# The softmax's division in a fused attention and two-MoE kernel: GpSimd's scaling of the exponentials against factors spread by TensorE

## The chip, the cores and the metric

The kernel runs on one core of a Trainium2 chip. The metric is device time in microseconds (us) of one execution, median of three runs. The engines are named as in the profile: PE is TensorE (PEld its weight loads), DVE is VectorE, ACT is ScalarE, POOL is GpSimd, SP is SyncE, which starts the DMAs.

## The reference

Three stages follow one another, all in float32. Attention runs over 2 batches x 12 heads x 448 positions x 64 columns with a causal mask; its output, 896 tokens of 768 columns, goes through two expert layers.

```python
scores = where(causal, q @ k.T / 8, -1e9)
attn = exp(scores - max(scores))
attn = attn / (sum(attn) + 1e-9)
x = (attn @ v), heads side by side            # 896 x 768
h = x @ w_in                                  # 768 -> 2048
x = (P(h) / (Q(h) + 1e-6)) @ w_out            # P cubic, Q quadratic; 2048 -> 768
out = (sigmoid(x @ w_gate) * (x @ w_val)) @ w_out2   # 768 -> 1536 -> 768
```

## The kernel before, in words

Attention works on 12 pairs of heads (2 batches x 6, `pairs`). A pair has 448 queries in four blocks of 112 (`NQ`), a block t against the t + 1 blocks of keys that the mask leaves; the blocks go in three groups, (0, 1), (2,) and (3,). For each block and each head j of the pair:

- `scores` (line 574): PE multiplies queries and keys into a PSUM tile s, both heads in different rows of the array.
- `maximum` (line 582): DVE adds the mask, scales, writes the tile e to SBUF and its extreme to sc.
- `exponentials` (line 596): ACT takes e to its exponential in place and the sums of the rows to `sum`.
- `inverses` (lines 602, 603): DVE adds 1e-9 to the sums of one group and takes the reciprocal, three times a pair.
- `normalised` (line 607): POOL multiplies e by its row's inverse sum, eight times a pair.
- `turn` (line 618): PE transposes e, block by block, into a PSUM tile p that shares its two buffers with s.
- `copied` (lines 626, 628): p goes to SBUF as pt, block 2 by ACT and the others by DVE.
- `values` (line 636): PE multiplies v and pt into x, 128 rows (two heads of 64 columns) x 448 queries, two PSUM buffers.
- `result_hi` (line 649) and `result_lo` (line 652): ACT rounds x to its high part xh, DVE subtracts, x - xh, to the low part xl. Every product of the expert layers is three products of high and low parts, for accuracy.

The first expert layer's products (`up`, lines 260 to 262, tile h; `out1_tile`, lines 319 to 321, tile o) begin as soon as a pair's xh and xl are there, and fill PE between the steps of attention. So do the portions of weights (`weight`: ACT lines 165 and 169, DVE line 172, POOL lines 180 and 184). What follows h is `rational` (lines 275 to 293, ACT, DVE, POOL).

The order on each engine is written out by a planner: every step is a job with an engine, a cost, the jobs it needs and a rank. `in_turn` walks through the jobs in a modelled time and lets each engine take the job of the lowest rank among those that are ready; the instructions are emitted in that order and each engine runs them in it. The tables R (ranks), C (added costs) and H (hand-over times) are numbers written into the kernel; expert products have rank 1000, so that they come where attention leaves PE free. From `late` on (all attention jobs done) the attention's memory is used for weights.

```python
job(("norm", n, t, j), "POOL", NORM[t] + C["norm"], [("inv", n, k)], rank + R["norm"], normalised, n, t, j)
deps = [("copy", n, t) for t in range(kt, NQ)] + [("x", n, kt - 1) if kt else ("lo", n - 2)]
job(("hi", n), "ACT", 0.42, [("x", n, NQ - 1)], rank + R["hi"], result_hi, n)
job(("lo", n), "DVE", 0.53, [("hi", n)], rank + R["lo"], result_lo, n)
```

Of the kernel before, what the change touches and what calls it, by code (L numbers as in the profile page):

```python
# [8 lines left out]
F32 = mybir.dt.float32  # L9
# [3 lines left out]
ALU = mybir.AluOpType  # L13
PSUM = bass.MemoryType.PSUM
# [57 lines left out]
def tile_causal_attention__moe_rational__moe_glu(  # L72
# [13 lines left out]
    nc = tc.nc  # L86


    B, NP, P, _, S = qk.shape
    CP, NQ, _, D = v.shape[2:]  # L90
# [29 lines left out]
    for i in range(N_WARM):  # L120
        nc.tensor.matmul(warm[:, : 2 * P], ones[:, :P], ones, start=True, stop=True)

    ident = const.tile([P, P], F32, name="ident")
# [4 lines left out]
        out=mask[:, S - CP :],  # L128
# [20 lines left out]
    xh = xpool.tile([P, KC, NT], F32R, name="xh")  # L149
    xl = xpool.tile([P, KC, NT], F32R, name="xl")  # L150
# [157 lines left out]
    def out1_tile(c, b, e):  # L308
# [37 lines left out]
        "p6": ("s2", "t2", "B", True),  # L346
        "p7": ("s3", "t3", "C", True),
        "p5": ("s1", "t1", "D", True),
        "p2": ("a12", "b21", "A", False),
        "p4": ("a22", "t4", "C", False),  # L350
        "p3": ("s4", "b22", "D", False),
# [110 lines left out]
    def combine(u, what):  # L462
# [11 lines left out]
        elif what == "u3":  # L474
            nc.vector.tensor_tensor(y, x, ps["C"], op=ALU.add)
        elif what == "c22":
# [3 lines left out]
        elif what == "c21":  # L480
            nc.vector.tensor_tensor(ps["C"], x, ps["C"], op=ALU.add)
        elif what == "pr1":
            nc.vector.tensor_tensor(z, z, ps["C"], op=ALU.mult)
        elif what == "c12":
# [45 lines left out]
    att = ExitStack()  # L530
    nat = att.enter_context(tc.tile_pool(name="nat", bufs=3))
    xn_p = att.enter_context(tc.tile_pool(name="xn", bufs=1))
# [1 line left out]
    pp = att.enter_context(tc.tile_pool(name="pp", bufs=2))  # L534
    st = att.enter_context(tc.tile_pool(name="st", bufs=3))
    ps_s = att.enter_context(tc.tile_pool(name="ps_s", bufs=2, space=PSUM))
    ps_x = att.enter_context(tc.tile_pool(name="ps_x", bufs=2, space=PSUM))

    pairs = [(b, hp) for b in range(B) for hp in range(NP)]
    T = {}  # L540

    GROUPS = [(0, 1), (2,), (3,)]
# [54 lines left out]
            e, e, AF.Exp, bias=d["sc"][:, t, j : j + 1], scale=-1.0, accum_out=d["sum"][:, t, j : j + 1]  # L597
        )

    def inverses(n, k):  # L600
        rs = T[n]["sum"][:, GROUPS[k][0] : GROUPS[k][-1] + 1]
        nc.vector.tensor_scalar_add(rs, rs, 1e-9)
        nc.vector.reciprocal(rs, rs)  # L603

    def normalised(n, t, j):
        e = T[n]["e", t, j]
        nc.gpsimd.tensor_scalar(e, e, T[n]["sum"][:, t, j : j + 1], 1.0, op0=ALU.mult, op1=ALU.mult)  # L607

    def turn(n, k):
        d = T[n]  # L610
# [9 lines left out]
    def copied(n, k, t):  # L620
# [6 lines left out]
        else:  # L627
            nc.vector.tensor_copy(dst, src)  # L628

    def values(n, kt):  # L630

        d = T[n]
        if kt == 0:
            d["x"] = ps_x.tile([P, 512], F32, tag="x", name=f"x_{n}")[:, :S]
        for j in range(2):
            nc.tensor.matmul(  # L636
                d["x"][j * D : (j + 1) * D, kt * CP :],
                d["v"][:, kt, j],
                d["pt"][:, j, kt * (PK + 1) : kt * PK + NQ].rearrange("p k c -> p (k c)"),
                start=(kt == 0),  # L640
                stop=(kt == NQ - 1),
            )

    def x_part(n):
        b, hp = pairs[n]
        return slice(None), hp, slice(b * S, (b + 1) * S)

    def result_hi(n):
        nc.scalar.copy(xh[x_part(n)], T[n]["x"])

    def result_lo(n):
        nc.vector.tensor_tensor(xl[x_part(n)], T[n]["x"], xh[x_part(n)], op=ALU.subtract)  # L652


    J = {}
# [1 line left out]
    def job(key, engine, cost, deps, rank, emit, *args):  # L657
        mode = MODES.get(key[0], "full") if engine == "PE" else None
        J[key] = Job(engine, cost, deps, rank, lambda: emit(*args), mode)
# [4 lines left out]
    def freed_by(ring, back=2):  # L664
        k = len(freed[ring]) - back
        return freed[ring][k] if k >= 0 else []
# [1 line left out]

    NG = len(GROUPS)
    LA = 2  # L670
    R = dict(s=-28.0, turn=-8.0, x=31.0, w=-6.0, max=-13.0, copy=-9.0, inv=-12.5, lo=20.0, norm=-12.0, hi=2.5, exp=8.25, e=2.0, p1=0.0, ts=0.0, th=0.0, tl=2.0, wh=-3.0, w2=-2.0, sum=-0.5)
    C = dict(w_at=14.0, w_step=6.0, s=0.05, p=-0.08, x=-0.03, max=0.05, exp=0.07, switch=0.19, stay=0, norm=0.0, copy=0.12, wa=-0.02)
    H = dict(PE=0.19, DVE=0.13, ACT=0.14, POOL=0.15, SP=0.15)
    MODES = {"s": "rows", "x": "columns"}
    EXP = (0.37, 0.465, 0.56, 0.65)
    MAX = (0.195, 0.31, 0.425, 0.54)
    NORM = (0.2, 0.32, 0.45, 0.57)
    COPY = (0.30, 0.53, 0.60, 1.0)
    both = range(2)
    for it in range(len(pairs) * NG + LA):  # L680
        n, k = divmod(it, NG)
        rank = it * NQ / NG
        if n < len(pairs):
            if k == 0:
                job(("load", n), "SP", 3.0, [("x", n - 3, NQ - 1)], (n - 2) * NQ, load, n)
            job(
                ("s", n, k),
                "PE",
                sum(0.187 * (t + 1) + 0.0 for t in GROUPS[k]) + C["s"],
                [("load", n), *freed_by("s")],  # L690
                rank + R["s"],
                scores,
                n,
                k,
            )
            for t in GROUPS[k]:
                for j in both:
                    job(("max", n, t, j), "DVE", MAX[t] + C["max"], [("s", n, k), ("p", n - 1, k)], rank + R["max"], maximum, n, k, t, j)
                    job(("exp", n, t, j), "ACT", EXP[t] + C["exp"], [("max", n, t, j), *[("norm", n - 3, t, i) for i in both]], rank + R["exp"], exponentials, n, t, j)
            freed["s"].append([("max", n, t, j) for t in GROUPS[k] for j in both])  # L700
        if it < LA:
            continue
        n, k = divmod(it - LA, NG)
        rank = (it - LA) * NQ / NG
        job(("inv", n, k), "DVE", 0.31, [("exp", n, t, j) for t in GROUPS[k] for j in both], rank + R["inv"], inverses, n, k)
        for t in GROUPS[k]:
            for j in both:
                job(("norm", n, t, j), "POOL", NORM[t] + C["norm"], [("inv", n, k)], rank + R["norm"], normalised, n, t, j)
        job(
            ("p", n, k),  # L710
            "PE",
            sum(0.191 * (t + 1) for t in GROUPS[k]) + C["p"],
            [("norm", n, t, j) for t in GROUPS[k] for j in both] + freed_by("s"),
            rank + R["turn"],
            turn,
            n,
            k,
        )
        for t in GROUPS[k]:
            job(("copy", n, t), "ACT" if t == 2 else "DVE", COPY[t] + C["copy"], [("p", n, k), ("x", n - 2, NQ - 1)], rank + R["copy"], copied, n, k, t)  # L720
        freed["s"].append([("copy", n, t) for t in GROUPS[k]])
        if k < NG - 1:
            continue
        for kt in range(NQ):
            deps = [("copy", n, t) for t in range(kt, NQ)] + [("x", n, kt - 1) if kt else ("lo", n - 2)]
            job(("x", n, kt), "PE", 0.187 * (NQ - kt) + C["x"], deps, rank + R["x"] + kt / 2, values, n, kt)
        job(("hi", n), "ACT", 0.42, [("x", n, NQ - 1)], rank + R["hi"], result_hi, n)
        job(("lo", n), "DVE", 0.53, [("hi", n)], rank + R["lo"], result_lo, n)


    def coefficients():
# [22 lines left out]
    UNIT2 = 0.525  # L754
    UNIT = {S: 0.615, CUT: 0.525, NT - CUT: 0.69}

    STAGES = [("SP", 4.0), ("ACT", 0.79 + C["wa"]), ("ACT", 0.79 + C["wa"]), ("DVE", 1.1), ("ACT", 0.73 + C["wa"]), ("POOL", 1.9)]
    portions = []
    held = {}

    def portion(key, w, free, rank):
        p = len(portions)
        portions.append(key)
        held[key] = [(*key, 3)], [(*key, 5)]
        for m, (engine, cost) in enumerate(STAGES):
            if m == 4 and key[0] in BY_POOL:
# [31 lines left out]
    def weights_in2(u):  # L798
        for q in range(2):
# [3 lines left out]
            w = weight2(u, q)  # L803
            for m, (engine, cost) in enumerate(STAGES[:4]):
                deps = [(*key, m - 1)] if m else [(*portions[p - 1], 0), *held[portions[p - 2]][0]]
# [70 lines left out]
    def followed(key, stages, rank, deps=()):  # L876

        free = [(*k, "after", m) for k, m in n_tmp[-3:-2]]
        free += [(*k, "after", 3) for k, _ in n_tmp[-2:-1]]
        follow(key, stages, rank, [*free, *deps])  # L880
        n_tmp.append((key, len(stages) - 1))
        freed["d"].append([(*key, "after", 3)])

    RATIONAL = [("ACT", 1.56), ("DVE", 1.75), ("ACT", 1.17), ("DVE", 1.8), ("ACT", 0.46), ("POOL", 1.15)]

    def scaled(stages, c, b, more=0.0):
        f = width(c, b) / S
        return [(engine, (cost - 0.15) * f + 0.15 + more) for engine, cost in stages]

    def stage_in(c, b):  # L890

        groups = [(0, 1), (2,), (3,)] if (c, b) == (0, 0) else [(i,) for i in range(NF)]
        for group in groups:
# [6 lines left out]
            for k in keys:  # L900
                followed(k, scaled(RATIONAL, c, b), ("out", c, b, 0, "mm", k[3]))
            yield
# [150 lines left out]
    latest = {}  # L1053
    for j in in_turn(J, {**H, "": 0.0}, C["switch"], C["stay"]):
        traced = nc.cur_bb.bb.instructions
# [54 lines left out]
```

## Time and profile before

| what | value |
|---|---|
| median of 3 runs | 597.2 us (596.33 to 599.57) |
| the profiled execution's own time | 596.2 us |
| its span, first to last instruction | 594.4 us |
| PE, DVE, ACT, POOL busy | 574.9, 448.0, 381.8, 359.3 us |
| mean granted clock of PE | 0.989 |
| read from HBM, written | 61.74 MB, 2.75 MB |

The profile is one execution. Busy times are sums of instructions; matmuls overlap in PE's pipeline, so PE can be busy without working at its peak. A row of a group gives busy time and mean of one instruction, then how long its engine had been idle before such instructions and who ended that. The chain of waits goes back from the last instruction to what released it. A PE product of f32 operands is two instructions in the profile (192 of line 636 for 96 products).

### The profile page before, as it was taken

Reading aid. Unit: us, or ns where it says so; the run is one execution under the profiler, and the core shown is the slowest. Engines: PE = TensorE matmul, PEld = TensorE weight load, DVE = VectorE, ACT = ScalarE, POOL = GpSimd, SP = SyncE. Lnnn points to the kernel's source line nnn. Section 1 sums busy time; section 2 is a strip of 40 time slices with the busy share of each in tenths; the row PEclk is TensorE's granted clock in tenths of the full one; section 3 lists DMA queues with packets and bytes.
Section 4 is the critical chain, followed back from the end, with each engine's and each line's share of the span. In section 5 each row is a group of like instructions: output and inputs, shape, how many; then the busy total and the mean of one; then the engine's idle time right before and its main releaser. Section 6 shows DMA issues by size and latency. Waiting matters only on the chain.

```text
span 594.4 us, 8892 instructions
## 1 busy us (share of the span) xinstructions
PE 574.9 (97%) x3052; PEld 490.3 (82%) x3052; DVE 448.0 (75%) x860; ACT 381.8 (64%) x755; POOL 359.3 (60%) x345
## 2 busy tenths in 40 slices
PE   7998999799999999999999989999999999999997
PEld 4554565478998998899889878999999999999997
DVE  4989999763986989699769995656667775767647
ACT  4886798574996958487658465687646655647210
POOL 3787756537757662836285887775657844856400
PEclk8898999899999999999999999999999999999999
DMA  7455431033442253313131103323443425341105
GB/s 245 159 194 184 139 109 48 16 107 107 159 160 70 90 160 106 108 53 108 53 107 54 53 2 106 116 97 110 156 160 109 129 86 158 118 135 66 55 0 187
DMA packets 35245, 65.06 MB, mean 109 GB/s; under 512 B 2368, under 2 KB 22592, under 8 KB 35200
## 3 DMA queue, kind: packets, MB, share of 16 engines
q1 hardware_dynamic: 35200, 64.50, 32.9%
q8 instruction: 24, 0.39, 0.3%
q14 instruction: 21, 0.17, 0.1%
HBM read 61.74 MB, written 2.75 MB: 108 GB/s over the span
## 4 chain that ended last, share of the span: by engine, by line
PE 83%; DVE 9%; POOL 3%; ACT 2%; issue 2%; POOLq 0%; DVEq 0%; ACTq 0%
PE o L319 6%; PE o L321 6%; PE o L320 6%; PE h L260 6%; PE h L261 6%; PE h L262 6%; PE z L512 5%; PE z L514 5%; PE z L513 5%; PE x L636 3%; PE p L618 2%; PE u_D L458 2%; PE u_D L459 2%; PE u_D L460 2%; PE u_C L459 2%; PE u_C L460 2%
## 5 line engine op out<-in xcount | busy, mean ns | idle before, releaser
L607 POOL TENSOR_SCALAR e<-e,sum 112x112 f32<-112x112 f32 (+3 forms) x96 | 54.5, 585 | 42.7 <-DVE sum L603 25.5
L423 POOL TENSOR_TENSOR room_a<-val,room_a 128x384 fp32r<-128x384 f32 x30 | 35.1, 1180 | 42.3 <-ACT room_a L419 34.7
L596 ACT ACTIVATE e<-e,sc 112x112 f32<-112x112 f32 (+3 forms) x96 | 49.8, 524 | 16.5 <-DVE sc L582 16.4
L184 POOL TENSOR_TENSOR ol_out<-val_out,oh_out 128x768 fp32r<-128x768 f32 x28 | 55.3, 1975 | 7.0 <-ACT oh_out L182 5.9
L512 PE MATMUL z<-oh_out,room_b 128*128 128x384 f32 x168 | 56.1, 334 | 0.0
L514 PE MATMUL z<-oh_out,room_b 128*128 128x384 f32 x168 | 56.1, 334 | 0.0
L513 PE MATMUL z<-ol_out,room_b 128*128 128x384 f32 x168 | 56.1, 334 | 0.0
L522 DVE TENSOR_TENSOR y<-y,z 128x384 f32<-128x384 f32 x84 | 44.4, 551 | 13.5 <-PE z L514 13.4
L423 POOL TENSOR_TENSOR room_a<-raw,room_a 128x384 fp32r<-128x384 f32 x38 | 45.2, 1207 | 10.9 <-ACT room_a L419 6.1
L582 DVE CUSTOM_DVE_ANT_0 e<-s,mask 112x112 f32<-112x112 f32 (+3 forms) x96 | 38.4, 444 | 9.2 <-PE s L574 8.0
L618 PEld LDWEIGHTS p<-ident,e 112*112 112x112 f32 x240 | 24.8, 139 | 24.7 <-POOL e L607 13.6
L172 DVE SCALAR_TENSOR_TENSOR val_out<-raw_out 128x768 uint32<-128x768 uint32 x28 | 36.3, 1297 | 10.8 <-POOL ol_out L184 5.2
L618 PE MATMUL p<-ident,e 112*112 112x112 f32 x240 | 34.7, 277 | 6.5 <-DVE pt L628 2.9
L293 POOL TENSOR_TENSOR room_a<-t_h,room_a 128x384 fp32r<-128x384 f32 (+1 forms) x16 | 17.0, 1060 | 35.8 <-ACT room_a L291 35.8
L574 PE MATMUL s<-qk 64*112 64x112 f32 (+3 forms) x192 | 33.5, 451 | 3.7 <-DVE sc L582 3.7
L321 PE MATMUL o<-room_b,ol_out 128*128 128x512 f32 (+1 forms) x96 | 36.9, 384 | 0.0
L320 PE MATMUL o<-room_b,oh_out 128*128 128x512 f32 (+1 forms) x96 | 36.9, 384 | 0.0
L319 PE MATMUL o<-room_b,oh_out 128*128 128x512 f32 (+1 forms) x96 | 36.8, 384 | 0.0
L261 PE MATMUL h<-xl,room_a 128*128 128x448 f32 (+2 forms) x96 | 35.0, 364 | 1.7 <-DVE xl L652 1.7
L260 PE MATMUL h<-xh,room_a 128*128 128x448 f32 (+2 forms) x96 | 36.3, 378 | 0.0
L395 DVE SCALAR_TENSOR_TENSOR val<-raw 128x768 uint32<-128x768 uint32 x24 | 24.1, 1005 | 15.9 <-ACT raw L392 15.6
L262 PE MATMUL h<-xh,room_a 128*128 128x448 f32 (+2 forms) x96 | 34.9, 364 | 0.0
(171 smaller groups left out, 1879.8 us busy)
## 6 DMA issues: line engine op xcount, KB each, us to landing
raw_out<-in_moe_w_out_dram SPq DMA_DIRECT2D x28, 768.0 KB, 4.2
raw_in<-in_moe_w_in_dram SPq DMA_DIRECT2D x16, 768.0 KB, 4.6
raw<-in_moe_w_gate_dram SPq DMA_DIRECT2D x24, 384.0 KB, 3.2
raw<-in_moe_w_val_dram SPq DMA_DIRECT2D x24, 384.0 KB, 3.9
qk<-in_qk_dram SPq DMA_DIRECT2D x12, 448.0 KB, 5.9
v<-in_v_dram SPq DMA_DIRECT2D x12, 224.0 KB, 3.1
out_dram<-y SPq DMA_DIRECT2D x14, 192.0 KB, 2.1
a_sb<-in_moe_a_dram SPq DMA_DIRECT2D x1, 2.0 KB, 7.5
```

The lines of the kernel that those rows point to most:

```text
L184: nc.gpsimd.tensor_tensor(lo, vf, hi, op=ALU.subtract)
L260: nc.tensor.matmul(ps, hi[:, c, fs], xh[:, c, bs], start=(c == 0), stop=False)
L261: nc.tensor.matmul(ps, hi[:, c, fs], xl[:, c, bs], start=False, stop=False)
L262: nc.tensor.matmul(ps, lo[:, c, fs], xh[:, c, bs], start=False, stop=(c == KC - 1))
L319: nc.tensor.matmul(ps, hi[:, es], gh, start=(i == 0), stop=False)
L320: nc.tensor.matmul(ps, hi[:, es], gl, start=False, stop=False)
L321: nc.tensor.matmul(ps, lo[:, es], gh, start=False, stop=(i == NF - 1))
L423: nc.gpsimd.tensor_tensor(lo, halves[u, PRODUCTS[name][0]], hi, op=ALU.subtract)
L512: nc.tensor.matmul(ps, gh[:, ms], hi[:, ns], start=(u == us[0]), stop=False)
L513: nc.tensor.matmul(ps, gh[:, ms], lo[:, ns], start=False, stop=False)
L514: nc.tensor.matmul(ps, gl[:, ms], hi[:, ns], start=False, stop=(u == us[-1]))
L618: nc.tensor.transpose(pz[:, j, at], e, ident[:CP, :CP])
```

## The change

The exponentials are no longer divided. Transposes and products with v work on them as they are, and x is scaled at the end. `inverses` runs once a pair over all its sums. A new step `factors` spreads the inverse sums over x's layout: for each block and head PE multiplies the column of 112 inverse sums, repeated 64 times, by the 112 x 112 identity, so that r holds at each of the 64 rows of a head the factor of each query. `factors_out` copies r from PSUM to SBUF on ACT, `result` multiplies it by x on DVE, and high and low parts are taken from the product. The low part goes from DVE to POOL, except in the last pair of each batch. x has one PSUM buffer and r the other. The ranks, costs and hand-over times of the planner are new.

```diff
-    ps_x = att.enter_context(tc.tile_pool(name="ps_x", bufs=2, space=PSUM))
+    ps_x = att.enter_context(tc.tile_pool(name="ps_x", bufs=1, space=PSUM))
+    ps_r = att.enter_context(tc.tile_pool(name="ps_r", bufs=1, space=PSUM))
...
-    def inverses(n, k):
-        rs = T[n]["sum"][:, GROUPS[k][0] : GROUPS[k][-1] + 1]
+    def inverses(n):
+        rs = T[n]["sum"]
         nc.vector.tensor_scalar_add(rs, rs, 1e-9)
         nc.vector.reciprocal(rs, rs)
-
-    def normalised(n, t, j):
-        e = T[n]["e", t, j]
-        nc.gpsimd.tensor_scalar(e, e, T[n]["sum"][:, t, j : j + 1], 1.0, op0=ALU.mult, op1=ALU.mult)
...
+    def factors(n):
+
+        d = T[n]
+        d["r"] = ps_r.tile([P, 512], F32, tag="r", name=f"r_{n}")[:, :S]
+
+        for i in range(NQ):
+            for j in range(2):
+                nc.tensor.matmul(
+                    d["r"][j * D : (j + 1) * D, i * CP : (i + 1) * CP],
+                    d["sum"][:, i, j : j + 1].to_broadcast([CP, D]),
+                    ident[:CP, :CP],
+                    start=True,
+                    stop=True,
+                )
+
+    def factors_out(n):
+        T[n]["xn"] = xn_p.tile([P, S], F32, tag="xn", name=f"xn_{n}")
+        nc.scalar.copy(T[n]["xn"], T[n]["r"])
...
+    def result(n):
+        nc.vector.tensor_tensor(T[n]["xn"], T[n]["xn"], T[n]["x"], op=ALU.mult)
+
     def result_hi(n):
-        nc.scalar.copy(xh[x_part(n)], T[n]["x"])
+        nc.scalar.copy(xh[x_part(n)], T[n]["xn"])
 
     def result_lo(n):
-        nc.vector.tensor_tensor(xl[x_part(n)], T[n]["x"], xh[x_part(n)], op=ALU.subtract)
+
+        eng = nc.vector if pairs[n][1] == NP - 1 else nc.gpsimd
+        eng.tensor_tensor(xl[x_part(n)], T[n]["xn"], xh[x_part(n)], op=ALU.subtract)
...
-    R = dict(s=-28.0, turn=-8.0, x=31.0, w=-6.0, max=-13.0, copy=-9.0, inv=-12.5, lo=20.0, norm=-12.0, hi=2.5, exp=8.25, e=2.0, p1=0.0, ts=0.0, th=0.0, tl=2.0, wh=-3.0, w2=-2.0, sum=-0.5)
-    C = dict(w_at=14.0, w_step=6.0, s=0.05, p=-0.08, x=-0.03, max=0.05, exp=0.07, switch=0.19, stay=0, norm=0.0, copy=0.12, wa=-0.02)
-    H = dict(PE=0.19, DVE=0.13, ACT=0.14, POOL=0.15, SP=0.15)
-    MODES = {"s": "rows", "x": "columns"}
+    R = dict(s=-41.5, turn=-13.0, r=-20.0, x=34.0, w=-3.5, max=-15.5, copy=-9.5, inv=7.0, xn=12.5, rout=-42.5, exp=6.75, hi=1.0, lo=4.5, e=3.0, p1=12.0, ts=0.0, th=-12.0, tl=0.0, wh=0.0, w2=-1.5, sum=6.0)
+    C = dict(w_at=9.0, w_step=5.0, s=0.3, p=0.1, x=0.15, max=0.08, exp=0.19, switch=0.0, stay=0, copy=0.0, wa=0.1, wd=0.2, xn=0.1, rat=0.2)
+    H = dict(PE=0.2, DVE=0.1, ACT=0.12, POOL=0.12, SP=0.03)
+    MODES = {"s": "rows", "x": "columns", "r": "columns"}
...
-                    job(("exp", n, t, j), "ACT", EXP[t] + C["exp"], [("max", n, t, j), *[("norm", n - 3, t, i) for i in both]], rank + R["exp"], exponentials, n, t, j)
+                    job(("exp", n, t, j), "ACT", EXP[t] + C["exp"], [("max", n, t, j), ("r", n - 3)], rank + R["exp"], exponentials, n, t, j)
...
-            [("norm", n, t, j) for t in GROUPS[k] for j in both] + freed_by("s"),
+            [("exp", n, t, j) for t in GROUPS[k] for j in both] + freed_by("s"),
...
+        job(("inv", n), "DVE", 0.4, [("exp", n, t, j) for t in range(NQ) for j in both], rank + R["inv"], inverses, n)
+        job(("r", n), "PE", 0.9, [("inv", n), ("r out", n - 1)], rank + R["r"], factors, n)
+        job(("r out", n), "ACT", 0.52, [("r", n), ("hi", n - 1), ("lo", n - 1)], rank + R["rout"], factors_out, n)
         for kt in range(NQ):
-            deps = [("copy", n, t) for t in range(kt, NQ)] + [("x", n, kt - 1) if kt else ("lo", n - 2)]
+            deps = [("copy", n, t) for t in range(kt, NQ)] + [("x", n, kt - 1) if kt else ("xn", n - 1)]
             job(("x", n, kt), "PE", 0.187 * (NQ - kt) + C["x"], deps, rank + R["x"] + kt / 2, values, n, kt)
-        job(("hi", n), "ACT", 0.42, [("x", n, NQ - 1)], rank + R["hi"], result_hi, n)
-        job(("lo", n), "DVE", 0.53, [("hi", n)], rank + R["lo"], result_lo, n)
+        job(("xn", n), "DVE", 0.52 + C["xn"], [("x", n, NQ - 1), ("r out", n)], rank + R["xn"], result, n)
+        job(("hi", n), "ACT", 0.57, [("xn", n)], rank + R["hi"], result_hi, n)
+        final = pairs[n][1] == NP - 1
+        job(("lo", n), "DVE" if final else "POOL", 0.62 if final else 1.14, [("hi", n)], rank + R["lo"], result_lo, n)
```

## Rows read from the trace of the kernel before

**Rows 1.** Totals of the page: engine, busy us, share of the span, instructions.

```profile
PE 574.9 (97%) x3052; PEld 490.3 (82%) x3052; DVE 448.0 (75%) x860; ACT 381.8 (64%) x755; POOL 359.3 (60%) x345
```

**Rows 2.** Engines by stretch: length, busy us of each, granted clock, DMA share, GB/s.

```profile
0.00:137.00 137.00, 123.79 (x762) 74.27 (x763) 111.75 (x349) 100.84 (x269) 82.50 (x127) 0.95 0.39 130
45.00:60.00 15.00, 13.29 (x77) 6.77 (x75) 14.86 (x34) 9.43 (x24) 10.65 (x17) 0.89 0.52 181
75.00:90.00 15.00, 15.00 (x95) 9.14 (x95) 14.22 (x42) 14.38 (x37) 7.86 (x14) 1.00 0.27 91
105.00:120.00 15.00, 11.46 (x67) 6.50 (x66) 11.85 (x40) 8.34 (x24) 7.36 (x10) 0.89 0.06 16
137.00:594.40 457.40, 451.06 (x2291) 416.04 (x2290) 336.21 (x511) 280.97 (x487) 276.82 (x219) 1.00 0.31 103
```

**Rows 3.** Chain that ended last: 0 to 137 us by line, then five pieces.

```profile
by line: PE x L636 11.0%; PE p L618 10.8%; PE s L574 8.8%; issue 7.8%; DVE e L582 7.7%; POOL e L607 7.3%; ACT e L596 5.9%; DVE pt L628 5.7%; DVE val_out L172 3.0%; PE warm L121 2.8%; PE o L319 2.5%; DVE sum L602 2.2%; PE o L320 2.1%; DVE va
...
51.69 2.09 issue
...
98.83 3.07 POOL e L607 x3
...
102.34 2.06 PE x L636 x16
...
110.44 3.31 POOL e L607 x3
...
114.20 3.69 PE x L636 x16
```

**Rows 4.** Waits, 0 to 137 us: who for whom, us, times, longest us.

```profile
PEld p L618 <- POOL e L607: 13.6, 27, 1.3
...
PE h L261 <- DVE xl L652: 1.7, 1, 1.7
```

**Rows 5.** Groups by line, 0 to 137 us: busy us, mean ns, idle before.

```profile
L607 POOL TENSOR_SCALAR e<-e,sum 112x112 f32<-112x112 f32 (+3 forms) x96 | 54.5, 585 | 42.7 <-DVE sum L603 25.5 <-ACT e L596 7.9 <-ACT d_h L285 2.8
...
L602 DVE TENSOR_SCALAR sum<-sum 112x2 f32<-112x2 f32 (+1 forms) x36 | 12.7, 351 | 1.9 <-ACT e L596 1.8
...
L652 DVE TENSOR_TENSOR xl<-x,xh 128x448 fp32r<-128x448 f32 x12 | 7.5, 621 | 8.3 <-ACT xh L649 8.3
...
L603 DVE RECIPROCAL sum<-sum 112x2 f32<-112x2 f32 (+1 forms) x36 | 6.1, 170 | 1.2
```

**Rows 6.** Timeline of DVE, then POOL, 49.5 to 54 us: start, us, instruction.

```profile
50.35 3.50 DVE L172 SCALAR_TENSOR_TENSOR val_out<-raw_out 128x768 uint32<-128x768 uint32 x1
...
50.00 1.26 POOL L607 TENSOR_SCALAR e<-e,sum 112x448 f32<-112x448 f32 x2
51.22 1.82 POOL L184 TENSOR_TENSOR ol_out<-val_out,oh_out 128x768 fp32r<-128x768 f32 x1
```

**Rows 7.** Single lines: duration ns min/median/max, first and last start us, forms.

```profile
L172 DVE SCALAR_TENSOR_TENSOR val_out<-raw_out x28: 945/1110/3504, 48.1 to 557.0; 128x768 uint32<-128x768 uint32 x28
...
L280 DVE TENSOR_TENSOR t_h<-t_h,h x32: 540/614/680, 79.3 to 321.1; 128x384 f32<-128x384 f32 x12, 128x512 f32<-128x512 f32 x12, 128x448 f32<-128x448 f32 x8
...
L447 DVE TENSOR_TENSOR room_b<-y,room_a x3: 1559/1576/1576, 344.1 to 350.0; 128x448 fp32r<-128x448 f32 x3
...
L329 ACT COPY y<-o x12: 512/534/553, 119.5 to 184.2; 128x448 f32<-128x448 f32 x12
...
L293 POOL TENSOR_TENSOR room_a<-t_h,room_a x16: 1016/1027/1152, 90.4 to 293.9; 128x384 fp32r<-128x384 f32 x12, 128x448 fp32r<-128x448 f32 x4
```

**Rows 8.** Timeline of PE, 88 to 98 us.

```profile
88.82 2.11 PE L636 MATMUL x<-pt,v 112*64 112x448 f32 x16
90.86 0.47 PE L260 MATMUL h<-xh,room_a 128*128 128x448 f32 x1
91.16 0.36 PE L261 MATMUL h<-xl,room_a 128*128 128x448 f32 x1
...
96.33 0.98 PE L618 MATMUL p<-ident,e 112*112 112x112 f32 x8
```

More of the change, by code (lines that the diff above doesn't have):

```diff
@@ L670, in tile_causal_attention__moe_rational__moe_glu @@
     LA = 2
-    R = dict(s=-28.0, turn=-8.0, x=31.0, w=-6.0, max=-13.0, copy=-9.0, inv=-12.5, lo=20.0, norm=-12.0, hi=2.5, exp=8.25, e=2.0, p1=0.0, ts=0.0, th=0.0, tl=2.0, wh=-3.0, w2=-2.0, sum=-0.5)
-    C = dict(w_at=14.0, w_step=6.0, s=0.05, p=-0.08, x=-0.03, max=0.05, exp=0.07, switch=0.19, stay=0, norm=0.0, copy=0.12, wa=-0.02)
-    H = dict(PE=0.19, DVE=0.13, ACT=0.14, POOL=0.15, SP=0.15)
-    MODES = {"s": "rows", "x": "columns"}
[L675 to L678, printed above, removed]
+    R = dict(s=-41.5, turn=-13.0, r=-20.0, x=34.0, w=-3.5, max=-15.5, copy=-9.5, inv=7.0, xn=12.5, rout=-42.5, exp=6.75, hi=1.0, lo=4.5, e=3.0, p1=12.0, ts=0.0, th=-12.0, tl=0.0, wh=0.0, w2=-1.5, sum=6.0)
+    C = dict(w_at=9.0, w_step=5.0, s=0.3, p=0.1, x=0.15, max=0.08, exp=0.19, switch=0.0, stay=0, copy=0.0, wa=0.1, wd=0.2, xn=0.1, rat=0.2)
+    H = dict(PE=0.2, DVE=0.1, ACT=0.12, POOL=0.12, SP=0.03)
+    MODES = {"s": "rows", "x": "columns", "r": "columns"}
+    EXP = (0.39, 0.48, 0.57, 0.67)
+    MAX = (0.28, 0.39, 0.51, 0.62)
+    COPY = (0.39, 0.62, 0.70, 1.09)
     both = range(2)
@@ L704, in tile_causal_attention__moe_rational__moe_glu @@
         rank = (it - LA) * NQ / NG
[L705 to L708, printed above, removed]
         job(
@@ L711, in tile_causal_attention__moe_rational__moe_glu @@
             "PE",
-            sum(0.191 * (t + 1) for t in GROUPS[k]) + C["p"],
-            [("norm", n, t, j) for t in GROUPS[k] for j in both] + freed_by("s"),
+            sum(0.2 * (t + 1) for t in GROUPS[k]) + C["p"],
+            [("exp", n, t, j) for t in GROUPS[k] for j in both] + freed_by("s"),
             rank + R["turn"],
@@ L755, in tile_causal_attention__moe_rational__moe_glu @@
     UNIT = {S: 0.615, CUT: 0.525, NT - CUT: 0.69}
-    STAGES = [("SP", 4.0), ("ACT", 0.79 + C["wa"]), ("ACT", 0.79 + C["wa"]), ("DVE", 1.1), ("ACT", 0.73 + C["wa"]), ("POOL", 1.9)]
+    STAGES = [("SP", 4.0), ("ACT", 0.79 + C["wa"]), ("ACT", 0.79 + C["wa"]), ("DVE", 1.1 + C["wd"]), ("ACT", 0.73 + C["wa"]), ("POOL", 1.9)]
     portions = []
@@ L882, in followed @@
         freed["d"].append([(*key, "after", 3)])
-    RATIONAL = [("ACT", 1.56), ("DVE", 1.75), ("ACT", 1.17), ("DVE", 1.8), ("ACT", 0.46), ("POOL", 1.15)]
+    RATIONAL = [(e, w + C["rat"]) for e, w in [("ACT", 1.56), ("DVE", 1.75), ("ACT", 1.17), ("DVE", 1.8), ("ACT", 0.46), ("POOL", 1.15)]]
     def scaled(stages, c, b, more=0.0):
```

## The prediction

> **What bounds the kernel now.** I read the totals first, then the engines by stretch, then the chain of waits, then the waits themselves. TensorE (PE) is busy 97% of the span, against 75% for VectorE (DVE), 64% for ScalarE (ACT) and 60% for GpSimd (POOL) [rows 1]. By stretch, the 457.4 us after 137 us hold only 6.3 us of PE idle time; that part is PE's own work and the change doesn't touch its arithmetic [rows 2]. So the change is worth what it is worth in the first 137 us, where the attention runs. There PE is idle for 13.2 us, DVE is busy 111.75 us, ACT 100.84, POOL 82.50 [rows 2]. The reader is to see three different conditions in it: from 45 to 60 us DVE is busy 14.86 of 15 us and PE waits; from 75 to 90 PE is busy for all of it, with products of the first MoE filling what attention leaves; from 105 to 120 no engine is full, and PE is idle for 3.5 us [rows 2]. The chain of that stretch names x, p and s on PE with 30.6%, maxima and copies on DVE, and POOL's division (line 607) with 7.3%, the adding of 1e-9 (line 602) with 2.2% [rows 3]. Its transposes waited 13.6 us in total for that division [rows 4].
>
> **Removed: division, two inverses in three.** POOL loses 96 instructions of 585 ns, 54.5 us [rows 5]. DVE loses 24 of 36 pairs of adding and reciprocal (351 and 170 ns) [rows 5]. Of this only what is on the chain can come back: 7.3% and 2.2% of 137 us are 10.0 and 3.0 us, 13.0 together [rows 3]. Next late, once the transposes wait for the exponentials alone, is ACT: its exponentials are on the chain with 5.9% already [rows 3], and a step that starts sooner often finds its PSUM buffer still being read. So the gain lies between 0 and 13.0; nothing in the trace tells how far ahead the other inputs were, and I take half, **-6.5 us**.
>
> **Removed: one stall.** At 50.35 us DVE's packing of a weight portion (line 172) took 3.50 us, where the shortest took 0.945; POOL ran two divisions from 50.00 to 51.26 and a subtraction from 51.22 to 53.04 at the same time [rows 6, 7]. The low part of a pair's output (line 652) stood behind it, and PE's product, which reads that part, waited: the chain has 2.09 us from 51.69 on that it puts down to no other instruction [rows 3]. After it the granted clock of the 15 us is 0.89 on average, between 1.2 and 2.4 GHz [rows 2]: 0.11 x 15 = 1.65 us more. Without the divisions this meeting doesn't come about in that form: **-3.7 us** (ends: 0, if POOL's weight work does the same alone, and 3.7).
>
> A rule bears on this. In the Trainium skill, SBUF — State Buffer, section Who interferes with whom, a VectorE instruction with two inputs in SBUF and a GpSimd instruction that reads SBUF exclude each other, the later one waiting to the end of the first. The row of 3.50 us agrees. It speaks against the term above: POOL's subtraction reads SBUF too and stays, so that by the rule only the two divisions' 1.26 us would come back, the clock's dip would stay, and the sum below would be -5.7 + 3.7 - 1.26 = -3.3, 592.9 us.
>
> **Added on PE.** Per pair the spreading is 4 blocks x 2 heads, and as each f32 product of x is issued as two instructions (192 for 96 products), 16 instructions of 112 columns. The 16 of one x move 4480 columns in 2.04 us from first start to the next instruction (88.82 to 90.86) [rows 8], so 0.455 ns a column; 16 x 112 columns are 0.82 us. Changing the form costs 0.1 us (the first h after x takes 0.47, the next 0.36) [rows 8]. 12 x 0.92 = 11.0 us. Bounds: 9.8 without the change of form; by a run of transposes, 8 in 0.98 us with its drain [rows 8], 12 x (16 x 0.1225 + 0.1) = 24.7. I take 11.0, since x has the same 64-column outputs. On the path it counts where PE itself is on the chain: x, p, s, warming and the two o rows shown, 38.0% [rows 3]: **+4.2 us** (ends 0 and 24.7). Beside the rest lie waits of PE that it fills.
>
> **Moved on DVE.** 12 multiplications, one input in PSUM, at 614 ns [rows 7] are +7.4 us; 10 subtractions of 621 ns [rows 5] leave, -6.2; 24 reciprocals -4.1. Net -2.9, and DVE's rows are 18.6% of the chain (e, pt, val_out, sum) [rows 3]: -0.5. Two subtractions stay on DVE, now with both inputs in SBUF; such a one took 1.576 us (line 447) [rows 7], so up to 2 x 0.95 = 1.9 more, +0.4 on the chain. Together **-0.1 us**.
>
> **Added on ACT.** 12 copies out of PSUM at 534 ns [rows 7] are 6.4 us. The copy to the high part only changes its input and is taken at its old price. With ACT's 5.9% of the chain **+0.4 us**; ends 0 and 6.4.
>
> **Costed at nothing.** Ten subtractions go to POOL at up to 1.152 us [rows 7], 11.5 us, which the 54.5 us removed leave room for; what hides them is that PE takes MoE products only when attention gives it nothing. Without that cover they are the slower rival below. The multiplication waits for the copied factors and for x; it holds ACT's high part and POOL's low part, and what stands behind it on DVE are the next pair's maxima, for which exponentials and transposes wait. x now has one PSUM buffer, and its next pair waits for the multiplication; but two x stood 11.9 us apart (102.34, 114.20) [rows 3] and the multiplication is 0.6. The one buffer of the factors makes ACT wait for the low part of the pair before, with the same 11.9 us of cover; were it gone, about 0.6 + 0.5 + 1.2 us a pair. No DMA is added, and the loads keep their condition. The order after 137 us is planned anew with the same work; there are 6.3 us of idle time to win or lose there, and I take 0 with 2 to each side.
>
> **Sum.** -6.5 - 3.7 + 4.2 - 0.1 + 0.4 = -5.7 us. Against the profiled execution's 596.2 us (span 594.4) that is 590.5; the median of the runs is 597.2, 1.0 above that execution. A measurement can tell about 0.5%, 3.0 us, from no change.
>
> **Rival 1, PE is the bound (no change).** For it: all 15 us from 75 to 90 are PE's [rows 2], and work that fills waits there must be done anyway. Against: 13.2 us idle, and much more in slow starts. The spreading is then paid in full, 11.0 in place of 4.2: +6.8, so 597.3.
>
> **Rival 2, the low part comes too late (slower).** The place is PE's h product that reads the low part, in a fixed order. High and low part now come after a multiplication (0.61), the low part takes 1.15 on POOL in place of 0.62, and may stand behind a weight subtraction of 1.82 [rows 6, 7]: 1.1 to 3.0 us later in each of ten pairs. One such wait cost 2.09 + 1.65 = 3.7 us. At 1.5 of them the gain is gone, from three on it is slower: -5.7 + 11.1 = +5.4, 601.6. For it: before, PE waited once for that line even with the quick subtraction (1.7 us, h on xl [rows 4]). Against: once in twelve pairs.
>
> **Rival 3, POOL was the whole trouble (far faster).** From 98.83 and 110.44 the chain stays 3.07 and 3.31 us on three divisions [rows 3], far over their mean of 585 ns, with a clock of 0.89 in the stretch around [rows 2]. If all 13.0 come back, the stall's 3.7 and that second 1.65: -18.35 + 4.2 + 0.3 = -13.9, 582.3. The section of the Trainium skill named above is the same reading: what POOL no longer reads, DVE no longer waits for.
>
> **How the numbers follow.** Forecast 0.44, with a range of its own of 587 to 594.2; rival 3 0.14; rival 1 0.22; rival 2 0.20. Rows speak for a gain, as POOL and DVE lose work in the stretch where they make PE wait; PE's full stretches keep it small. Faster by over 0.5% (under 594.2): 0.44 + 0.14 = 0.58. Same: 0.22. Slower: 0.20. The range goes from rival 3's 582 to rival 2's 601.6 with the upper part of the 2 us after 137: 603; further waits and more idle time won are left out, under 0.2.
>
> **What would show it.** Right: the last attention x ends about 6 us sooner; no POOL in the chain's attention part but weights; r near 11 us of PE time by starts; DVE's line 602 some 4 us; POOL near 40 us in 0 to 137; no val of 3.5 us beside POOL. Rival 1: 45 to 120 us with PE busy throughout and the same end. Rival 2: h on xl from POOL among PE's waits, several times, each with a lower clock behind it. Rival 3: a clock of 1.00 in all stretches after the first 20 us. Wrong altogether: a change after 137 us larger than that before it, or the multiplication and the factors' copy on the chain in most pairs.

## The result and the profile after

The changed kernel takes **591.55 us** (four runs, 591.18 to 591.77), the kernel before 598.2 us in the runs beside it. The ratio is **0.989**, 95% interval 0.9858 to 0.9922: faster by 1.1%. The profiled execution took 591.18 us with a span of 589.4, 5.0 us less than the 594.4 of before.

The totals of the page after (engine, busy us, share, instructions), and the granted clock in 40 slices of the span, first before, then after:

```profile
PE 576.6 (98%) x3244; PEld 497.3 (84%) x3244; DVE 441.7 (75%) x814; ACT 388.3 (66%) x767; POOL 320.6 (54%) x259
```

```profile
PEclk8898999899999999999999999999999999999999
```

```profile
PEclk9999999999999999999999999999999999999999
```

The line of before has a third dip that no term of the prediction names, in the first 30 us: the mean granted clock of before was 0.89 and 0.88 there, as the rows below show, and is 1.00 after. What that is worth is not separated.

```profile
0.00:15.00 15.00, 10.84 (x56) 7.16 (x56) 6.57 (x35) 7.24 (x23) 5.22 (x17) 0.89 0.77 243
15.00:30.00 15.00, 14.42 (x88) 7.87 (x86) 13.51 (x41) 12.21 (x34) 11.21 (x16) 0.88 0.50 164
```

The engines by stretch after, with the columns of [rows 2]:

```profile
0.00:137.00 137.00, 133.30 (x995) 88.99 (x996) 103.55 (x306) 108.65 (x285) 53.54 (x47) 1.00 0.43 142
45.00:60.00 15.00, 15.00 (x124) 9.56 (x123) 10.94 (x38) 13.02 (x37) 6.74 (x6) 1.00 0.48 149
75.00:90.00 15.00, 15.00 (x123) 10.21 (x120) 13.40 (x37) 12.18 (x36) 4.66 (x4) 1.00 0.50 171
105.00:120.00 15.00, 14.61 (x127) 9.31 (x125) 13.40 (x36) 13.15 (x33) 4.84 (x4) 1.00 0.01 2
137.00:589.40 452.40, 443.30 (x2250) 408.29 (x2249) 338.15 (x509) 279.69 (x482) 267.08 (x212) 1.00 0.30 101
```

Against [rows 2], PE's idle time in the first 137 us fell from 13.2 to 3.7 us, POOL's work from 82.5 to 53.5, DVE's from 111.8 to 103.6; ACT's rose from 100.8 to 108.7. The two stretches with a mean clock of 0.89 now stand at 1.00. The stretch after 137 us has 9.1 us of PE idle time instead of 6.3.

Waits after, 0 to 137 us, and the groups of the new steps, answering to [rows 4, 5]:

```profile
PEld p L615 <- ACT e L597: 5.2, 9, 0.8
...
ACT xn L644 <- POOL xl L673: 3.1, 2, 2.4
```

```profile
L673 POOL TENSOR_TENSOR xl<-xn,xh 128x448 fp32r<-128x448 f32 x10 | 13.3, 1329 | 17.0 <-ACT xh L668 17.0
...
L634 PE MATMUL r<-ident,sum 112*64 112x112 f32 x192 | 11.8, 265 | 0.0
...
L665 DVE TENSOR_TENSOR xn<-xn,x 128x448 f32<-128x448 f32 x12 | 7.3, 612 | 2.7 <-ACT xn L644 1.9 <-PE x L652 0.8
...
L644 ACT COPY xn<-r 128x448 f32<-128x448 f32 x12 | 6.3, 528 | 3.9 <-POOL xl L673 3.1 <-PE r L634 0.7
...
L603 DVE TENSOR_SCALAR sum<-sum 112x8 f32<-112x8 f32 x12 | 3.7, 305 | 0.0
```

The chain that ended last, followed back, reaches no step of the attention any more; its part in the first 137 us begins at 121.8 and lies on weights:

```profile
by line: DMA raw_in<-in_moe_w_in_dram 3.2%; DVE val_in L172 2.6%; issue 2.3%; POOL room_b L184 1.4%; ACT raw_in L165 0.7%; POOL room_b L180 0.6%; ACT raw_in L169 0.6%; POOLq L180 0.0%; DVEq L172 0.0%; ACTq L165 0.0%
```

The transposes' 13.6 us of waiting for POOL became 5.2 us of waiting for the exponentials. PE's own waits name no low part any more.

Where the time came from is seen by following the same work through both traces (PE's timeline, by starts). The last attention product ends at 120.4 us instead of 135.4, but fewer expert products are done by then (81 instructions of h and o, not 114). The 145th such instruction, the first h of the second chunk, starts at 133.2 instead of 141.5: **8.3 us** are won by there, the spreading included. The first u of the second layer starts at 337.0 instead of 344.0 (7.0 ahead), the last z at 584.8 instead of 590.0 (**5.2 ahead**). So some 3 us are given back after the attention, 1.3 in the first expert layer and 1.8 in the second.

### The profile page after: what moved, and what is told of

Read it like the earlier page. It is cut to its first block, busy times and chain, and to the rows that moved or that the text cites. A ratio compares the mean times of both kernels' runs of the same rounds, so it can differ in the third digit from the quotient of the medians.

```text
span 589.4 us, 9051 instructions
## 1 busy us (share of the span) xinstructions
PE 576.6 (98%) x3244; PEld 497.3 (84%) x3244; DVE 441.7 (75%) x814; ACT 388.3 (66%) x767; POOL 320.6 (54%) x259
## 4 chain that ended last, share of the span: by engine, by line
PE 66%; DVE 5%; ACT 3%; DMA 2%; POOL 1%; issue 1%; ACTq 0%; POOLq 0%; DVEq 0%
PE z L512 5%; PE z L514 5%; PE z L513 5%; PE o L320 5%; PE o L321 5%; PE o L319 5%; PE h L262 4%; PE h L261 4%; PE h L260 4%; PE u_C L458 2%; PE u_C L459 2%; PE u_C L460 2%; PE u_D L460 2%; PE u_D L459 2%; PE u_D L458 2%; PE u_A L460 2%
## 5 line engine op out<-in xcount | busy, mean ns | idle before, releaser
L184 POOL TENSOR_TENSOR ol_out<-val_out,oh_out 128x768 fp32r<-128x768 f32 x28 | 52.9, 1890 | 6.9 <-ACT oh_out L182 5.5
L514 PE MATMUL z<-oh_out,room_b 128*128 128x384 f32 x168 | 56.1, 334 | 0.0
L513 PE MATMUL z<-ol_out,room_b 128*128 128x384 f32 x168 | 56.1, 334 | 0.0
L293 POOL TENSOR_TENSOR room_a<-t_h,room_a 128x384 fp32r<-128x384 f32 (+1 forms) x16 | 19.7, 1232 | 52.5 <-ACT room_a L291 46.0
L172 DVE SCALAR_TENSOR_TENSOR val_out<-raw_out 128x768 uint32<-128x768 uint32 x28 | 34.7, 1241 | 10.7 <-ACT raw_out L169 5.6
L293 POOL TENSOR_TENSOR room_b<-t_h,room_b 128x512 fp32r<-128x512 f32 (+1 forms) x16 | 20.7, 1291 | 34.7 <-ACT room_b L291 33.8
L165 ACT ACTIVATE raw_out<-raw_out 128x768 f32<-128x768 f32 x28 | 25.6, 916 | 14.0 <-DMA raw_out<-in_moe_w_out_dram 13.8
L260 PE MATMUL h<-xh,room_b 128*128 128x384 f32 (+1 forms) x96 | 34.7, 362 | 0.0
L262 PE MATMUL h<-xh,room_b 128*128 128x384 f32 (+1 forms) x96 | 34.7, 362 | 0.0
```

What stands on the lines that cost most here:

```text
L184: nc.gpsimd.tensor_tensor(lo, vf, hi, op=ALU.subtract)
L260: nc.tensor.matmul(ps, hi[:, c, fs], xh[:, c, bs], start=(c == 0), stop=False)
L262: nc.tensor.matmul(ps, lo[:, c, fs], xh[:, c, bs], start=False, stop=(c == KC - 1))
L513: nc.tensor.matmul(ps, gh[:, ms], lo[:, ns], start=False, stop=False)
L514: nc.tensor.matmul(ps, gl[:, ms], hi[:, ns], start=False, stop=(u == us[-1]))
```

## The experiments

Ratios are taken against runs of the kernel before made beside each experiment, 597.3 to 597.6 us in the median.

**Division left out** (in the kernel before, order on every engine unchanged; the output stays undivided)

```diff
     def normalised(n, t, j):
         e = T[n]["e", t, j]
-        nc.gpsimd.tensor_scalar(e, e, T[n]["sum"][:, t, j : j + 1], 1.0, op0=ALU.mult, op1=ALU.mult)
+        return
```

> The kernel before with GpSimd's 96 multiplications left out and everything else, order included, as it was (the output stays undivided; the inverses are still made). Theory A, the division was a link of the chain and a reader of SBUF beside VectorE: 6 to 12 us less than before, 586 to 592, with the granted clock at 1.00 from 45 to 60 us. Theory B, the gain of the change is the new order of the planner and not the division: less than 2 us, 596 or more.

Measured: 586.26 us, ratio 0.981 (0.9782 to 0.9837), **-11.0 us**. Theory A holds against B; its two halves, link of the chain and reader beside DVE, are not told apart by this run. By stretch, and DVE's adding of 1e-9 in this run:

```profile
0.00:137.00 137.00, 127.03 (x816) 83.23 (x817) 109.60 (x354) 104.82 (x277) 39.05 (x37) 0.99 0.42 142
45.00:60.00 15.00, 13.07 (x96) 7.36 (x95) 14.47 (x42) 10.55 (x31) 7.97 (x6) 1.00 0.57 202
105.00:120.00 15.00, 14.51 (x100) 9.87 (x97) 11.55 (x40) 11.94 (x30) 1.13 (x1) 1.00 0.31 106
```

```profile
L602 DVE TENSOR_SCALAR sum<-sum 112x2 f32<-112x2 f32 (+1 forms) x36 | 10.1, 280 | 1.9 <-ACT e L596 1.8
```

The clock stays up from 45 to 60 and from 105 to 120 us. DVE's adding went from 12.7 us [rows 5] to 10.1 only, where 36 of its shortest (157 ns in this run) would be 5.7, so most of its stretched durations have another cause than the division. From 45 to 60 us DVE is busy 14.47 of 15 us, and where PE's weight loads wait for another engine in 0 to 137 us, it is for DVE's maxima and copies most, no longer for POOL:

```profile
PEld s L574 <- DVE sc L582: 8.3, 13, 1.5
...
PEld x L636 <- DVE pt L628: 3.7, 3, 2.0
PEld p L618 <- ACT e L596: 3.5, 6, 0.9
```

In this run the last z starts 10.9 us earlier than before, the 145th instruction of h and o as well: nothing is given back later with the old order.

**The same multiplications put back beside** (in the changed kernel; they read and write a spare tile, and nobody waits for them)

```diff
+    spare = st.tile([CP, S], F32, tag="spare", name="spare", bufs=1)
+    nc.gpsimd.memset(spare, 0.0)
+
+    def beside(n, t, j):
+        nk = (t + 1) * CP
+        nc.gpsimd.tensor_scalar(spare[:, :nk], spare[:, :nk], T[n]["sc"][:, t, j : j + 1], 1.0, op0=ALU.mult, op1=ALU.mult)
...
+                    job(("beside", n, t, j), "POOL", 0.0, [("exp", n, t, j)], rank - 12.0, beside, n, t, j)
```

> The changed kernel, the same order on all engines, with 96 multiplications of the old sizes put back on GpSimd on a spare tile that nobody waits for. Theory A1, the division cost time as a link of the chain: within 1.5 us of the changed kernel, 590 to 593. Theory A2, it cost time because GpSimd's reads of SBUF shut VectorE out: half of the gain or more goes, 595 to 600, and VectorE's line of 1e-9 and the packing of weights show single durations over 1.5 us more often.

Measured: 595.34 us, ratio 0.9952 (0.9936 to 0.9968), 3.8 us more than the changed kernel. The size is A2's, but the sign that A2 named is missing: DVE's busy time in 0 to 137 us is 103.95, as good as unchanged, and the longest adding of 1e-9 took 1.14 us (1.79 in the changed kernel). Who waited for the low part in this run:

```profile
  ACT xn L651: 10.4, 7
  PEld h L261: 2.2, 2
  PE h L261: 1.7, 2
```

The low part stood behind the spare multiplications in POOL's queue. The copy of the next factors waited for it (3.1 us before, 10.4 now), and PE's h, which had not waited at all, waited twice.

**Low parts on VectorE**, without and with the spare multiplications

```diff
-        eng = nc.vector if pairs[n][1] == NP - 1 else nc.gpsimd
-        eng.tensor_tensor(xl[x_part(n)], T[n]["xn"], xh[x_part(n)], op=ALU.subtract)
+        nc.vector.tensor_tensor(xl[x_part(n)], T[n]["xn"], xh[x_part(n)], op=ALU.subtract)
...
-        final = pairs[n][1] == NP - 1
-        job(("lo", n), "DVE" if final else "POOL", 0.62 if final else 1.14, [("hi", n)], rank + R["lo"], result_lo, n)
+        job(("lo", n), "DVE", 0.62, [("hi", n)], rank + R["lo"], result_lo, n)
```

> The changed kernel with all twelve low parts on VectorE, as in before, none on GpSimd. Theory Q, the slower low part on GpSimd keeps TensorE and the copy of the factors waiting: 588 to 590.5. Theory D, VectorE's 6.2 us more cost as much as GpSimd's: 591 to 592.5. Theory V, VectorE is the bound: 594 or more.

> All low parts on VectorE, and the 96 multiplications put back on GpSimd on a spare tile; the order is otherwise that of the run with low parts on VectorE (596.1). On GpSimd only weights and the function behind h are left to be delayed. Theory Q, the 3.8 us that the spare multiplications cost the changed kernel came from low parts standing behind them in GpSimd's queue: within 1.5 us of 596.1. Theory A2, they came from GpSimd's reads shutting VectorE out: 599 or more.

Measured: 596.07 us, ratio 0.9974 (0.9958 to 0.9991), and 598.73 us, ratio 1.0005 (0.9986 to 1.0025). The first has theory V's time, 4.5 us above the changed kernel, but not its mechanism. The edit also moves the job in the planner, so the order on every engine is another one from the first low part on. PE's 80th instruction of h and o starts at 117.1 us in this run and at 117.0 in the changed kernel, and about 1 us more of attention is left to do then. Most of the loss comes in the 7.5 us after, in the changed kernel first and then in this run:

```profile
117.50:125.00 7.50, 7.50 (x56) 6.19 (x56) 4.07 (x5) 4.86 (x9) 4.78 (x3) 1.00 0.61 193
117.50:125.00 7.50, 4.31 (x42) 2.92 (x40) 6.42 (x13) 5.91 (x10) 1.05 (x1) 1.00 0.00 1
```

PE stands still for 3.2 us there, 2.1 of them before an x; the copied block pt that x reads was finished by DVE at 120.4, behind steps of the function of h. The first products o wait twice more. In the new order the 72nd h starts at 108.3 us instead of 99.8, so that function falls beside the last pair. How much of the 4.5 us is DVE's added work and how much the other order is not separated.

The second run has the first one's order. It lies between its two expectations, 2.7 us above the first, with intervals that overlap a little, so the time alone doesn't decide. The engines in the first 137 us, without and then with the spare multiplications, and the adding of 1e-9 in the same two runs:

```profile
0.00:137.00 137.00, 130.39 (x973) 85.34 (x974) 106.01 (x315) 108.61 (x284) 38.90 (x37) 1.00 0.42 141
```

```profile
0.00:137.00 137.00, 128.28 (x963) 83.29 (x964) 110.47 (x315) 107.30 (x282) 100.33 (x133) 1.00 0.41 137
```

```profile
L603 DVE TENSOR_SCALAR sum<-sum 112x8 f32<-112x8 f32 x12 | 3.0, 250 | 0.0
```

```profile
L603 DVE TENSOR_SCALAR sum<-sum 112x8 f32<-112x8 f32 x12 | 5.4, 447 | 0.0
```

DVE needs 4.5 us more for the same instructions beside a busy POOL. Of that 2.4 is the adding of 1e-9, which has one tensor input, and 2.4 are low parts, weight packing and steps of the function of h with two inputs in SBUF (the low parts 8.7 us instead of 7.9); the other lines are 0.3 shorter together, copies out of PSUM and maxima among them. So both ways of disturbing are seen: queueing in POOL, when something urgent stands there, and stretched DVE instructions. The Trainium skill's rule on two inputs in SBUF (SBUF — State Buffer, Who interferes with whom), by which such an instruction and a GpSimd one that reads SBUF exclude each other, agrees with the two-input part of the second. How much of the 2.7 us is due to stretching is not settled.

**Factors once, and factors twice** (in the changed kernel; in the first run eleven pairs take the first pair's factors, in the second every pair's are multiplied twice into the same place)

```diff
         d = T[n]
+        if n:
+            d["r"] = T[0]["r"]
+            return
         d["r"] = ps_r.tile([P, 512], F32, tag="r", name=f"r_{n}")[:, :S]
```

```diff
-        for i in range(NQ):
+        for i in (*range(NQ), *range(NQ)):
             for j in range(2):
                 nc.tensor.matmul(
```

> The changed kernel with the factors spread for the first pair alone; the other eleven copies read that tile again (11 of 12 pairs get the wrong factors). TensorE loses 11 x 0.98 = 10.8 us. Theory P, TensorE is now the bound of the attention: 8 to 11 us less, 581 to 583.5. Theory W, as forecast, TensorE fills waits with it: 3 to 5 us less, 586.5 to 588.5.

> The changed kernel with every pair's factors multiplied twice into the same place, 12 x 0.98 = 11.8 us more on TensorE. Theory P, TensorE is the bound: 9 to 12 us more, 600.5 to 603.5. Theory W: 3 to 5 us more, 594.5 to 596.5.

Measured: 589.73 us, ratio 0.9874 (0.9847 to 0.9902), 1.8 us under the changed kernel with overlapping intervals; and 600.59 us, ratio 1.0053 (1.0038 to 1.0068), **9.0 us** over it. By starts on PE's timeline one spreading takes 0.91 us (10.9 in twelve), the second dose 0.76 more (9.1 in twelve). So neither theory held on both sides: of the first dose 1.8 of some 10 us is paid at the end (2.8 by the 145th instruction of h and o, 130.4 against 133.2), of the second nearly all. PE was just short of full. The stretch of 105 to 120 us without the factors, and that of 30 to 45 us with the double dose:

```profile
105.00:120.00 15.00, 12.49 (x73) 7.74 (x72) 11.23 (x23) 9.84 (x22) 5.48 (x3) 0.89 0.17 54
```

```profile
30.00:45.00 15.00, 15.00 (x145) 9.89 (x141) 9.96 (x31) 11.77 (x37) 6.03 (x6) 1.00 0.50 172
```

Without the factors PE idles for 2.5 us in that stretch and its mean clock is 0.89 there; by 0.11 x 15 us, an estimate, that takes back up to 1.65 us of the gain, so the first dose alone may cost more than 1.8. With the double dose PE is full and DVE drops to 9.96 of 15 us.

**The planner's numbers exchanged** (the steps that both kernels have take the other's ranks, costs and hand-over times)

```diff
-    R = dict(s=-41.5, turn=-13.0, r=-20.0, x=34.0, w=-3.5, max=-15.5, copy=-9.5, inv=7.0, ...)
+    R = dict(s=-28.0, turn=-8.0, r=-20.0, x=31.0, w=-6.0, max=-13.0, copy=-9.0, inv=7.0, ...)
-    C = dict(w_at=9.0, w_step=5.0, s=0.3, p=0.1, x=0.15, max=0.08, exp=0.19, switch=0.0, ...)
+    C = dict(w_at=14.0, w_step=6.0, s=0.05, p=-0.08, x=-0.03, max=0.05, exp=0.07, switch=0.19, ...)
...
```

> The changed kernel ordered with the ranks, costs and hand-over times of before, wherever before has one (new steps keep theirs). Theory A, the edit itself carries the gain: 589 to 595, faster than before. Theory B, the planner's new numbers carry it: 597 or more.

> The kernel before, division on GpSimd and all, ordered with the ranks, costs and hand-over times of the changed one, wherever that has one. Theory A: no gain, 597 to 606. Theory B, the new numbers carry the gain: 590 to 594.

Measured: 604.04 us, ratio 1.0111 (1.0091 to 1.0131), and 606.12 us, ratio 1.0145 (1.0116 to 1.0175). Both are slower than the kernel before. Neither theory as written holds: the edit needs its own order, and that order does nothing for the old kernel. In the changed kernel with the old numbers the attention is over at 122.1 us, but then PE stands still; its waits and the last stretch:

```profile
PE o L319 <- ACT room_a L291: 4.4, 1, 4.4
PE o L320 <- POOL room_a L293: 4.3, 1, 4.3
```

```profile
120.00:137.00 17.00, 8.27 (x41) 6.01 (x38) 7.62 (x10) 5.15 (x10) 9.17 (x8) 0.74 0.14 45
```

The last of the 72 instructions of h of the first chunk starts at 122.5 us (99.8 in the changed kernel) and the first o right behind it at 122.7 (105.4), so the function between them, which o needs, has no work of PE to hide behind, and the clock falls as well.

**Ranks or costs** (the exchange above, one half at a time)

> The changed kernel with the ranks of before (for the steps that before has), the new costs and hand-over times kept. With all planner numbers of before it took 604.0, its attention ended at 122.1 us, but the last first-layer products h came so late that TensorE waited 8.7 us for the function behind them. Theory K, the modelled costs set where h goes between the attention's steps: most of the 12.5 us come back, 591 to 596. Theory R, the ranks do it: 600 or more.

> The changed kernel with the costs and hand-over times of before, the new ranks kept. Theory K, the costs set it: 600 or more, with the waits of o for the last function behind h as in the run with all old numbers. Theory R, the ranks: 591 to 596.

Measured: with the old ranks 594.69 us, ratio 0.9952 (0.9936 to 0.9967); with the old costs 605.82 us, ratio 1.0135 (1.0111 to 1.0159). Theory K: with the costs and hand-over times of before the attention ends at 111.5 us with 33 instructions of h and o done (81 in the changed kernel), the last h of the first chunk starts at 119.9, the first o at 126.8, and PE's longest wait is again o:

```profile
PE o L319 <- DVE t_h L281: 6.5, 1, 6.5
```

The lower modelled costs put the attention's steps ahead of h; those of the changed kernel leave room for h between them. Which of the costs does it was not tried. The ranks are worth 3.1 us.

**What is given back later.** Two runs changed ranks of the later part alone: all eight (e, p1, ts, th, tl, wh, w2, sum) as before, then p1 alone.

```diff
-    R = dict(..., e=3.0, p1=12.0, ts=0.0, th=-12.0, tl=0.0, wh=0.0, w2=-1.5, sum=6.0)
+    R = dict(..., e=2.0, p1=0.0, ts=0.0, th=0.0, tl=2.0, wh=-3.0, w2=-2.0, sum=-0.5)
```

> The changed kernel with the eight ranks that order only what comes after the attention (e, p1, ts, th, tl, wh, w2, sum) as in before. The changed kernel is 8.3 us ahead at its 288th expert product and 5.0 at the end. Theory L, these ranks give the 3.3 us back: 588 to 589.5. Theory M, an earlier start of the same work meets the same limits there: 591 to 592.5.

> The changed kernel with one rank as in before, p1 = 0 in place of 12: ScalarE's steps of the second expert layer come earlier. In the changed kernel TensorE waits twice 1.5 us there for ScalarE (u_A and u_C), where before it waited once 1.5 us for VectorE and 0.3 for ScalarE. If that rank is behind the 1.8 us lost there: 589 to 590.5; if not, 591 to 592.5.

Measured: 592.27 us, ratio 0.9914 (0.9896 to 0.9933), and 592.65 us, ratio 0.9917 (0.9896 to 0.9939): no gain. In the second, the waits are those of the changed kernel, whose PE waits after 137 us are:

```profile
PE u_A L458 <- ACT x L471: 1.5, 1, 1.5
PE u_C L458 <- ACT z L479: 1.5, 1, 1.5
PE u_C L459 <- DVE room_b L447: 0.9, 1, 0.9
PE o L320 <- POOL room_b L293: 0.7, 1, 0.7
PE o L319 <- ACT room_b L291: 0.3, 1, 0.3
```

That is 4.9 us against 2.3 before (u_C for DVE y 1.5, for POOL 0.5, u_A 0.3). It is where the time goes back: 1.0 at o in the first expert layer, 1.6 more at u in the second. In the first run the second part does come back: from the first u to the last z it takes 245.5 us (before 246.0, after 247.8), and the waits at u are nearly those of before (1.5 and 0.5). But PE waits 1.7 us at 323.7 for an o that needs POOL's room_b, and in the 3.3 us from 326.6 its granted clock is 0.50; the first u starts 4.2 us later than in the changed kernel. So the eight ranks carry the loss of the second layer, p1 alone doesn't, and an order that avoids both losses was not found.

## Why the prediction was right, point by point

The forecast of -5.7 us, to 590.5, met -5.0 in the profiled executions and -1.1% in the ratio. Its terms fared differently. What was removed came out nearly as said (-10.2 forecast, -11.0 in the run without division), and all that the change adds cost 5.3 us (586.26 to 591.55) against a forecast of 4.5. Within that 4.5 two errors nearly cancelled: the spreading stood there with 4.2, and leaving it out gave 1.8; the 3.1 us lost after the attention stood there with nothing. So close a sum is in part luck.

- **The division on the chain and the stall.** I had -6.5 and -3.7, together -10.2, for the division and two inverses in three. The division alone gave -11.0. Sum and cause were right; that half of the chain's 13.0 would come back was a guess, and how the 11.0 fall to its two terms is not measured. The dip from 45 to 60 us went as foreseen; that from 105 to 120 stood in rival 3 alone, the one in the first 30 us nowhere. What is late next was wrong: I named ACT, in the run without division PE waits mostly for DVE.
- **The spreading on PE.** 11.0 us of PE time was right (10.9). I put +4.2 on the path; taking it away gives 1.8 at the end, with a dip of the clock that takes some of the gain back. The reason given, that it fills waits, holds; PE's share of the old chain overstated what of it is paid.
- **DVE, -0.1.** No run measures this term by itself. The move of ten subtractions was valued at their 6.2 us times DVE's 18.6% of the chain, 1.2 us. Putting them back cost 4.5, but with another order, and the trace puts the loss at the end of the attention, where 3.2 us of PE standing still fall into 7.5 us; until 117 us the two runs are level within about 1 us, so the 1.2 is neither confirmed nor refuted.
- **ACT, +0.4.** Twelve copies of the factors took 6.3 us (6.4 forecast). What they cost on the path was not tried alone.
- **Costed at nothing.** The low part on POOL cost PE no wait in the changed kernel, as said, though it took 1.33 us in the mean instead of at most 1.152. This rests on POOL's being half empty: with the 96 multiplications back, h waited, and the mechanism of rival 2 appeared.
- **The order.** I priced only the order after 137 us, at 0 with 2 to each side; there some 3 us went. The order inside the attention I did not price at all. The planner's new numbers, which make both, are worth 12.5 us (604.0 against 591.55), more than the whole gain. The sum came out because they fit the new work; the rows of before could not show that, and this too is luck.
- **Rivals.** Rival 1 is half true: PE is full from 30 to 105 us after the change, yet the time fell, since it is full of work that had been waiting. Rival 3's sign came, a clock of 1.00 in every stretch, without its 582 us: of the 18.35 us that it took for the removal 11.0 came in the run without division, and what was added cost 5.3 in place of its 4.5. Rival 2's sign, h waiting for the low part, did not come.
- **The signs.** r took 10.9 us, the adding 3.7, no packing of an output weight more than 1.94, as said. The last attention x ended 15.0 us sooner and not 6, as fewer expert products lie between. POOL had 53.5 us in 0 to 137 and not near 40, since four portions of one weight buffer come there instead of one (9.2 us more) and the low parts are slower. The chain after, which begins at 121.8 us on weights, can't say whether the multiplication or the factors' copy holds the attention.
- **The Trainium skill's rule.** By the rule of SBUF — State Buffer (Who interferes with whom) taken alone I worked out 592.9, with only the divisions' 1.26 us back and the clock's dip staying. The run without division has the old order and tells: its longest packing of an output weight still takes 2.44 us, beside POOL's subtraction, so 1.06 us of the 3.50 came back, near what the rule gives. But h waits 0.4 us there for the low part and not 1.7, and the dip went, which the rule's sum had staying.

## What to carry to other kernels

A share of the chain is an upper end for what removing a link gave here (the division's 10.0 us and the stall's 3.7 are 13.7, and 11.0 came), but it doesn't price work that is added afterwards: 38% of the spreading's 11 us was forecast, and less was paid. An engine that is just short of full takes one dose of extra work nearly free and pays for the second in full, so it is worth doubling a suspected cost as well as removing it. An edit that lets a planner order everything anew measures two things at once, and the trace has to say where the time was lost. When a static order was made with modelled costs, shortening one stage without renewing these costs can turn a gain into a loss: look at which filler work is left behind when the stage ends.

## What was not expected of the hardware

PE's clock fell in the run that gave PE less to do: without eleven of twelve spreadings the mean granted clock was 0.89 from 105 to 120 us, where the changed kernel had 1.00 with PE busy 14.61 of 15 us. In finer stretches of that run, PE first stood still for 1.8 us, worked on at the full 2.4 GHz, and then ran at 1.2 GHz for 3.3 us though it was busy throughout:

```profile
105.20:107.00 1.80, 0.04 (x2) 0.05 (x2) 1.76 (x7) 1.48 (x6) 0.74 (x1) 1.00 0.00 0
107.00:108.70 1.70, 1.61 (x10) 0.80 (x10) 1.59 (x4) 1.67 (x6) 0.40 (x1) 1.00 0.00 0
108.80:112.10 3.30, 3.30 (x12) 1.26 (x12) 3.21 (x8) 1.41 (x5) 0.00 (x0) 0.50 0.03 7
```

In the kernel before, h waited 1.7 us from 52.7 and the clock was 0.50 from 56.1 to 59.4. Such a wait alone doesn't settle it: with the low parts on VectorE PE waited 2.1 us from 118.4 and the clock stayed at 1.00. The busy time of a stretch misleads here. From 45 to 60 us PE was busy 13.29 us before [rows 2] and 13.07 without the division, but at half the clock its instructions take longer: before did 77 of them, the run without division 96.
